# New tables for a planned order: half-width turns of three blocks, earlier and later ranks of weight conversions, twelve tiles with their rests by identity products

## The chip, the cores and the metric

The kernel runs on one core of one Trainium2 chip. The metric is the device time of one execution in microseconds (us). In the rows PE is TensorE, PEld is TensorE's loading of stationary operands, DVE is VectorE, ACT is ScalarE, POOL is GpSimd and SP is SyncE, which issues all the transfers here.

## What is computed

An attention of the mLSTM kind (a recurrence with a matrix state) over 4 sequences of 768 steps with 8 heads of width 40 gives 3072 rows of 320 numbers. Two dense layer pairs of inner width 2048 follow, each with its own pointwise function.

```python
def _attn_ref(q, k, v, i_gate, f_gate, o_gate):      # per step t
    m_new = np.maximum(f_gate[:, :, t] + m, i_gate[:, :, t])
    C = f_stab[:, :, None, None] * C + i_stab[:, :, None, None] * np.einsum('bhd,bhe->bhde', vt, kt)
    ...
    y[:, :, t] = o * h_tilde / denom

def _moe_ref(x, w_in, w_out):
    h = x @ w_in                    # 3072x320 @ 320x2048
    g = np.where(h >= 1, h, np.where(h <= -1, 0.0, (h + 1) ** 2 / 4))
    return g @ w_out                # 3072x2048 @ 2048x320

def _moe2_ref(x, w_in, w_out):
    h = x @ w_in
    g = np.maximum(h, 0.0) ** 2
    return g @ w_out
```

## The kernel before

**Tiling.** The 3072 rows are cut into 24 chunks of 128. The attention of a chunk needs the state of the chunk before it in the same sequence. Chunks are put together to blocks: for the first dense pair (part 0) three blocks of two chunks and six of three (`SIZES1`), for the second (part 1) eight of three. The inner width 2048 is 16 tiles of 128 (`f` from 0 to 15). One visit is a block with one `f`: `mm1` (L694) makes `h`, ScalarE and VectorE make the activation (L699, L705, L712), its value is split into a rounded part `g0` (L270) and a rest `g1` (L722), and `mm2` (L747) adds the block's products with the output weights to one accumulator per chunk.

**Weights.** They arrive as 64-bit floats, one transfer of 704 KB per tile and part (`raw`, L284), and become a float32 in five steps: `a_abs` on ScalarE (L288), then four VectorE instructions (L296, L297, L301, L309). `a_hi` (L270) writes the rounded weights. Their rest, the float32 less the rounded value, is made in one of two ways. Either VectorE makes it by two subtractions (`v_lo` L318 and `lo` L322, the latter sometimes on GpSimd). Or, for the tiles of part 0 that are named in `PLO`, TensorE makes it in two halves (`plo`, L345): the float32 by an identity matrix (L350), less the rounded value by a negated identity (L351), in an accumulator from which ScalarE copies (L270).

**Order.** Nothing is ordered by hand. Each step is handed to a planner (`Plan`) with its engine or a choice of engines, a rank, a cost, what it needs and what it makes; the planner plays the program through with these costs, takes the ready step of lowest rank on each engine, and the instructions are issued in the order that comes out. On each engine they then run in that order. Tables of numbers set the ranks:

- `TURNS1` and `TURNS2`: in what order some blocks take ranges of `f`. A block that leaves off in the middle of the width keeps its partial sums in `pa` (`keep`, and L762 where there are sums already) and adds them at the end (L775).
- `AT`: ranks of the first six attentions; `LEAD1`: how many visits ahead of a block its later attentions stand.
- `WAT`: ranks of the 16 weight conversions of part 0; `WLEAD2`: how many visits ahead of their use those of part 1 stand, for `f` under 8 and from 8 on.
- `GATE`: rank of the gates of the later chunks. The first six attentions (`SPR`) get their decay factors by a spread on TensorE (L504), the others by a transfer (`fb`).
- `GLOV`: blocks whose `g1` is made on VectorE; for the others the planner chooses between GpSimd and VectorE.
- `wraw`, `d0`, `d1` in `bufs`: how many buffers the raw weights and the decay matrices have.
- `FILL`: 140 products of zeros (L815) of lowest rank, which the planner puts where TensorE has nothing else to do.

Of the attention, L509 is the scan that makes a decay matrix `d`, L537 the scores, L518 the scores times `d`, L572 the outer products, L582 and L586 the state, L609 and L613 the reading of the state and of the scores, L633 the result `xn`, L652 and L662 its transpose and the rest of its rounding.

## Time and profile before

| what | us |
|---|---|
| median of three runs | 897.83 (895.91 to 904.17) |
| the profiled execution, its own time | 893.81 |
| its span, first to last instruction | 892.0 |
| TensorE's matmuls busy in the span | 873.6 (98%) |
| TensorE's weight loads busy | 850.4 (95%) |
| VectorE, ScalarE, GpSimd busy | 451.9, 451.5, 390.0 |

A busy time is the time covered by an engine's instructions in the profile. Matmuls overlap and their ends are modelled, so that a busy TensorE need not be at its peak. A row of a window gives the busy time of each engine in it, with the number of instructions, and the granted share of TensorE's clock.

### The profile page before, as it was taken

The page shows a single profiled execution, that of the slowest core. Times are in us where ns is not written, and L with a number is a line of the kernel's source. Part 1 is how long each engine was busy: PE and PEld are TensorE (multiplying, and loading weights), DVE is VectorE, ACT ScalarE, POOL GpSimd, SP SyncE. Part 2 cuts the span into 40 slices and gives each one's busy share as a digit, 9 for nine tenths or more (in the row PEclk, how much of TensorE's full clock was granted, in tenths as well). Part 3 has the DMA queues.
Part 4 walks back from the last instruction along what each step waited for, and adds up shares of the span by engine and source line. Part 5 has one row for each costly group of instructions (what it writes and reads, how often), then busy time and mean ns, then how long its engine had stood idle before and what let it go on. Part 6 is the DMA issues. An engine that isn't in the chain of part 4 may idle for free.

```text
span 892.0 us, 15463 instructions
## 1 busy us (share of the span) xinstructions
PE 873.6 (98%) x5922; PEld 850.4 (95%) x5922; DVE 451.9 (51%) x806; ACT 451.5 (51%) x973; POOL 390.0 (44%) x383
## 2 busy tenths in 40 slices
PE   8889999999999999999999999999999999999997
PEld 7768999999999999999999999999999999999997
DVE  5798898864535444454528888722222222211221
ACT  5256596555454554544468675543344444333433
POOL 3221433465646555555435556533333333333333
PEclk7699999999999999999999999999999999999999
DMA  7654445373233233343102332001101010000000
GB/s 234 201 193 147 151 144 166 114 208 105 88 108 113 94 118 100 98 130 101 51 1 70 134 127 87 1 18 39 34 25 34 22 38 10 23 12 12 16 9 22
DMA packets 55981, 75.74 MB, mean 85 GB/s; under 512 B 7252, under 2 KB 44792, under 8 KB 55908
## 3 DMA queue, kind: packets, MB, share of 16 engines
q1 hardware_dynamic: 55908, 74.77, 26.4%
q8 instruction: 46, 0.75, 0.4%
q14 instruction: 27, 0.22, 0.1%
HBM read 65.90 MB, written 8.85 MB: 84 GB/s over the span
## 4 chain that ended last, share of the span: by engine, by line
PE 90%; DVE 5%; ACT 2%; issue 1%; DMA 1%; POOL 1%; DVEq 0%; ACTq 0%; POOLq 0%
PE h L694 38%; PE acc L747 36%; PE v L613 4%; PE s L537 3%; PE v L572 2%; PE s L504 2%; PE s L652 2%; PE v L609 1%; PE acc L815 1%; PE acc L350 1%; DVE wt L301 1%; DVE wt L296 1%; DVE r L712 1%; DVE wt L309 1%; ACT r L699 1%
## 5 line engine op out<-in xcount | busy, mean ns | idle before, releaser
L722 POOL TENSOR_TENSOR g<-r,g 128x384 fp32r<-128x384 f32 (+1 forms) x256 | 262.4, 1026 | 368.9 <-ACT g L270 292.4
L747 PE MATMUL acc<-w,g 128*128 128x320 f32 x2304 | 380.5, 311 | 0.7 <-POOL g L722 0.5
L694 PE MATMUL h<-xTh,w 128*128 128x384 f32 (+1 forms) x1360 | 356.9, 331 | 2.8 <-DVE r L712 2.3
L747 PEld LDWEIGHTS acc<-w,g 128*128 128x128 f32 x2304 | 349.6, 188 | 4.5 <-POOL g L722 1.2
L694 PE MATMUL h<-xTl,w 128*128 128x384 f32 (+1 forms) x816 | 266.5, 327 | 0.0
L694 PEld LDWEIGHTS h<-xTh,w 128*128 128x128 f32 x1360 | 242.7, 188 | 6.5 <-DVE r L712 4.9
L270 ACT ACTIVATE g<-r 128x384 fp32r<-128x384 f32 (+1 forms) x272 | 136.2, 503 | 108.4 <-DVE r L714 61.0
L714 DVE TENSOR_TENSOR r<-r,h 128x384 f32<-128x384 f32 x128 | 70.6, 553 | 236.8 <-ACT r L701 236.8
L694 PEld LDWEIGHTS h<-xTl,w 128*128 128x128 f32 x816 | 153.9, 189 | 0.0
L699 ACT ACTIVATE r<-h,half 128x384 f32<-128x384 f32 (+1 forms) x144 | 78.2, 543 | 117.3 <-PE h L694 114.3
L701 ACT ACTIVATE r<-h 128x384 f32<-128x384 f32 x128 | 62.6, 489 | 137.3 <-PE h L694 99.3
L712 DVE SCALAR_TENSOR_TENSOR r<-r,h 128x384 f32<-128x384 f32 (+1 forms) x144 | 72.3, 503 | 91.1 <-ACT r L705 87.3
L705 ACT ACTIVATE r<-r 128x384 f32<-128x384 f32 (+1 forms) x144 | 70.0, 486 | 3.0
L509 DVE TENSOR_TENSOR_SCAN d<-fb,csb 128x512 f32<-128x512 f32 x36 | 48.6, 1349 | 33.8 <-PE v L613 31.5
L544 POOL TENSOR_TENSOR vt<-vko,it 128x369 f32<-128x369 f32 x24 | 28.9, 1206 | 61.9 <-PE v L613 49.3
L613 PEld LDWEIGHTS v<-vt,d 128*128 128x128 f32 x384 | 49.4, 198 | 1.0 <-DVE C L582 0.4
L613 PE MATMUL v<-vt,d 128*128 128x41 f32 x384 | 49.1, 279 | 0.2 <-DVE C L582 0.2
L518 DVE TENSOR_TENSOR d<-s,d 128x512 f32<-128x512 f32 x48 | 31.0, 674 | 18.3 <-PE s L537 18.3
L301 DVE SCALAR_TENSOR_TENSOR wt<-wraw,wt 128x704 int32<-128x704 int32 x32 | 37.4, 1172 | 0.2
L309 DVE SCALAR_TENSOR_TENSOR wt<-wraw,wt 128x704 int32<-128x704 int32 x32 | 33.9, 1058 | 0.1
L537 PE MATMUL s<-qk 40*128 40x128 f32 x384 | 32.1, 303 | 1.2 <-DVE rc L623 1.0
L288 ACT ACTIVATE wt<-wraw 128x704 f32<-128x704 f32 x32 | 27.0, 844 | 11.4 <-DMA wraw<-in_wts_dram 4.5
(73 smaller groups left out, 633.8 us busy)
## 6 DMA issues: line engine op xcount, KB each, us to landing
wraw<-in_wts_dram SPq DMA_DIRECT2D x32, 704.0 KB
vko<-in_vko_dram SPq DMA_DIRECT2D x24, 524.5 KB
fb<-f SPq DMA_DIRECT2D x18, 512.0 KB
qk<-in_qk_dram SPq DMA_DIRECT2D x48, 160.0 KB
x<-x SPq DMA_DIRECT2D x24, 192.0 KB
x<-o SPq DMA_DIRECT2D x24, 160.0 KB
out_dram<-o SPq DMA_DIRECT2D x24, 160.0 KB
qh<-in_qh_dram SPq DMA_DIRECT2D x20, 180.0 KB
```

The lines of the kernel that those rows point to most:

```text
L270: nc.scalar.activation(out=out, in_=in_, func=ACTF.Copy)
L509: nc.vector.tensor_tensor_scan(out=d.rearrange("p h t -> p (h t)"), data0=(z["fb"][a] if spr else z["fb"][:, 4 * a:4 * a + 4]).rearrange(" ...
L537: nc.tensor.matmul(out=z["s", a][:, h], lhsT=z["qk"][r, 0, h], rhs=z["qk"][r, 1, h], start=True, stop=True)
L613: nc.tensor.matmul(out=z["y"][:, E * h:E * (h + 1)], lhsT=z["d", a][:, h - 4 * a], rhs=z["vt"][:, h], start=(h == 0 and c == 0), stop=True ...
L694: nc.tensor.matmul(out=h, lhsT=a, rhs=b, start=(i == 0), stop=(i == 7))
L699: nc.scalar.activation(out=r, in_=z["h"], func=ACTF.Relu, scale=0.5, bias=half)
L701: nc.scalar.activation(out=r, in_=z["h"], func=ACTF.Relu)
L705: nc.scalar.activation(out=z["r"], in_=z["r"], func=ACTF.Square)
L712: nc.vector.scalar_tensor_tensor(out=r, in0=r, scalar=1.0, in1=z["h"], op0=ALU.min, op1=ALU.max)
L714: nc.vector.tensor_mul(out=r, in0=r, in1=z["h"])
L722: engine[e].tensor_sub(out=z["g1"], in0=z["r"], in1=z["g0"].bitcast(F32))
L747: nc.tensor.matmul(out=acc[k][:, 0:DM], lhsT=a, rhs=b, start=(f == f0 and i == 0), stop=(f == f1 - 1 and i == 2))
```

## The change

Tables alone are changed in effect. The first three blocks take their turns by eight `f` and no longer by four, so that a block leaves off once and not three times. The ranks of the first attentions, of the conversions and of the gates move. `PLO` goes from the 8 even tiles to 12. The `g1` of blocks 1, 2 and 3 is made on VectorE, that of block 0 where the planner chooses. Raw weights have three buffers, not four, and the decay matrices two, not one. `EARLY` is 0, so that the new places it selects (`xy`, the tag `h`) are not taken, and a spread's tile keeps its shape.

```diff
-TURNS1 = [(0, 0, 4), (1, 0, 4), (0, 4, 8), (1, 4, 8), (2, 0, 4), (2, 4, 8),
-          (0, 8, 12), (1, 8, 12), (2, 8, 12), (0, 12, 16), (1, 12, 16), (2, 12, 16)]
+TURNS1 = [(0, 0, 8), (1, 0, 8), (2, 0, 8), (0, 8, 16), (1, 8, 16), (2, 8, 16)]
...
-AT = [-20, -16, -8, -4, 4, 8]
-WAT = [-14, -13, -12, -11, -3, -2, -1, 0, 11, 12, 13, 14, 20, 21, 22, 23]
-LEAD1 = {3: [12, 8, 4], 4: [12, 8, 4], 5: [12, 8, 4], 6: [12, 8, 4], 7: [12, 8, 4], 8: [8.5, 6, 3.5]}
+AT = [-21.0, -17.0, -5.5, -3.0, 3.5, 6.5]
+WAT = [-14, -13.0, -13, -6, -3, 0, 2, 2.5, 9.5, 17.5, 16.5, 25.0, 27.0, 27.0, 31.5, 32.0]
+LEAD1 = {3: [12.5, 8, 3.5], 4: [13.5, 5.5, 3.5], 5: [13.5, 10, 7.0], 6: [13, 6.5, 2.5], 7: [13, 11, 3.0], 8: [7.5, 5, 2.5]}
...
-GATE = -14
+XTB, PAB = 3, 6
+RAWB, DB = 3, 2
+EARLY = 0
+GATE = -19
...
-PLO = range(0, 16, 2)
-WLEAD2 = (10, 10)
+PLO = (0, 1, 2, 3, 4, 6, 8, 10, 11, 12, 13, 14)
+WLEAD2 = (13, 6)
...
-GLOV = (0,)
+GLOV = (1, 2, 3)
...
-        wraw=4, wt=3, qk=2, vko=2, fb=1, qh=2, ab=2, d0=1, d1=1,
+        wraw=RAWB, wt=3, qk=2, vko=2, fb=1, qh=2, ab=2, d0=DB, d1=DB,
```

In the changed file the lines stand one or two further down: L296 is L297, L301 is L302, L712 is L714, L694 is L696.

The first place is VectorE's queue ahead of the first activation of a dense visit (`r<-r,h`). Before, these are the rows up to it, with the conversion of a seventh tile (`wt_582`) and of an eighth (`wt_662`):

```order
L518 TENSOR_TENSOR d1_684<-s_696,d1_684 128x512
L633 TENSOR_TENSOR xn_716<-v_657,sg_409 128x320
L309 SCALAR_TENSOR_TENSOR wt_582<-wraw_511,wt_582 128x704
L296 TENSOR_SCALAR wt_662<-wt_662 128x704
L297 TENSOR_SCALAR wt_662<-wt_662 128x704
L582 TENSOR_TENSOR C_741<-v_720,csb_84 120x369
L662 TENSOR_TENSOR xTl_737<-s_726,xTh_736 128x3x128
L301 SCALAR_TENSOR_TENSOR wt_662<-wraw_558,wt_662 128x704
L712 SCALAR_TENSOR_TENSOR r_591<-r_591,h_571 128x256
```

In the changed kernel the same activation has these rows ahead of it, with the sixth tile (`wt_541`) as the last, and the seventh (`wt_603`) behind it:

```order
L310 SCALAR_TENSOR_TENSOR wt_541<-wraw_496,wt_541 128x704
L511 SCALAR_TENSOR_TENSOR d0_646<-s_623,csb_81 128x512
L511 SCALAR_TENSOR_TENSOR d1_657<-s_641,csb_81 128x512
L319 TENSOR_TENSOR w5_655<-wt_541,w5_655 64x128
L323 TENSOR_TENSOR w5_655<-wt_541,w5_655 128x576
L625 TENSOR_SCALAR rc_684<-v_650 128x8
L626 TENSOR_TENSOR rc_684<-v_650,rc_684 128x8
L627 RECIPROCAL rc_684<-rc_684 128x8
L714 SCALAR_TENSOR_TENSOR r_586<-r_586,h_563 128x256
...
L297 TENSOR_SCALAR wt_603<-wt_603 128x704
```

Two conversions, among other rows, have moved from ahead of the first activation to behind it.

The second place is TensorE's queue behind the fourth visit of block 0. Before, block 1 begins with tile 0 there (its transposed input is `xTh_736`):

```order
L747 MATMUL acc0_789<-w2_489,g0_834 128x320 x2
L747 MATMUL acc0_789<-w2_489,g1_845 128x320
L504 MATMUL s_854<-w11_122,csb_84 128x128 x4
L747 MATMUL acc1_795<-w2_489,g0_834 128x320 x2
L747 MATMUL acc1_795<-w2_489,g1_845 128x320
L694 MATMUL h_869<-xTh_736,w0_381 128x256
```

In the changed kernel block 0 (`xTh_415`) goes on with tile 4 instead, and ahead of it stand products of zeros and an identity half of tile 6:

```order
L696 MATMUL h_798<-xTh_415,w3_526 128x256 x2
L696 MATMUL h_798<-xTl_416,w3_526 128x256
L817 LDWEIGHTS x2_125
L817 MATMUL acc2_131<-x2_125 128x160
L817 LDWEIGHTS x2_125
L817 MATMUL acc2_131<-x2_125 128x160
L351 MATMUL acc2_131<-wt_603,csb_81 128x352
L352 MATMUL acc2_131<-w6_809,nident_82 128x352
...
L696 MATMUL h_836<-xTh_415,w4_608 128x256
```

Of the 140 products of zeros all stand ahead of the first visit before, and 118 in the changed kernel; the other 22 stand between the first and the ninth.

The third place is SP's queue of transfers, where the raw weights of tiles 0 to 2 have been asked for. Before, the load of tile 3 (`wraw_335`) stands behind the inputs of the third attention:

```order
L463 DMA qk_302<-in_qk_dram 40x2x512 x2
L467 DMA vko_317<-in_vko_dram 128x1049
L284 DMA wraw_335<-in_wts_dram 128x1408
L436 DMA a1_91<-w10_123 36x640
L476 DMA qh_372<-in_qh_dram 120x384
L463 DMA qk_376<-in_qk_dram 40x2x512 x2
L467 DMA vko_392<-in_vko_dram 128x1049
```

In the changed kernel it (`wraw_397`) stands behind those of the fourth too:

```order
L465 DMA qk_299<-in_qk_dram 40x2x512 x2
L469 DMA vko_311<-in_vko_dram 128x1049
L437 DMA a1_88<-w10_120 36x640
L478 DMA qh_338<-in_qh_dram 120x384
L473 DMA fb_342<-f1_87 128x8x128
L465 DMA qk_362<-in_qk_dram 40x2x512 x2
L469 DMA vko_379<-in_vko_dram 128x1049
L285 DMA wraw_397<-in_wts_dram 128x1408
```

The load of tile 3 has moved behind five more transfers.

## Rows read from the trace of the kernel before

**Rows 1.** Windows, by stage: busy us of PE, PEld, DVE, ACT, POOL, then granted clock

```profile
0.00:40.00 40.00, 35.33 (x215) 30.71 (x215) 25.31 (x44) 16.59 (x30) 11.15 (x15) 0.66 0.65 209
40.00:80.00 40.00, 34.10 (x241) 28.40 (x240) 36.51 (x67) 22.21 (x48) 9.93 (x10) 0.91 0.63 198
80.00:200.00 120.00, 118.57 (x930) 113.44 (x931) 102.67 (x196) 75.64 (x193) 52.40 (x59) 1.00 0.49 153
200.00:600.00 400.00, 398.13 (x2731) 391.33 (x2731) 220.34 (x376) 221.35 (x463) 211.34 (x195) 1.00 0.27 86
600.00:892.00 292.00, 287.43 (x1811) 286.46 (x1809) 67.05 (x125) 115.67 (x241) 105.20 (x104) 1.00 0.07 23
```

**Rows 2.** Timeline of ScalarE and VectorE, first 200 us: start us, us, instruction

```profile
52.12 0.48 ACT L699 ACTIVATE r<-h,half 128x256 f32<-128x256 f32 x1
...
71.13 0.41 DVE L712 SCALAR_TENSOR_TENSOR r<-r,h 128x256 f32<-128x256 f32 x1
...
197.18 0.42 DVE L712 SCALAR_TENSOR_TENSOR r<-r,h 128x256 f32<-128x256 f32 x1 [1.61 <-ACT r L705]
```

**Rows 3.** Groups of VectorE by line and shape, first 200 us: count | busy, mean ns | idle before

```profile
L301 DVE SCALAR_TENSOR_TENSOR wt<-wraw,wt 128x704 int32<-128x704 int32 x19 | 20.3, 1070 | 0.1
...
L309 DVE SCALAR_TENSOR_TENSOR wt<-wraw,wt 128x704 int32<-128x704 int32 x19 | 18.6, 980 | 0.0
L509 DVE TENSOR_TENSOR_SCAN d<-s,csb 128x512 f32<-128x512 f32 x12 | 14.7, 1223 | 9.0 <-PE s L504 5.4 <-PE v L613 3.6
L518 DVE TENSOR_TENSOR d<-s,d 128x512 f32<-128x512 f32 x20 | 12.9, 681 | 3.3 <-PE s L537 3.3
L296 DVE TENSOR_SCALAR wt<-wt 128x704 f32<-128x704 f32 x19 | 12.2, 642 | 0.0
L297 DVE TENSOR_SCALAR wt<-wt 128x704 int32<-128x704 int32 x19 | 12.1, 635 | 0.7
...
L722 DVE TENSOR_TENSOR g<-r,g 128x256 fp32r<-128x256 f32 x16 | 8.6, 536 | 1.2 <-ACT g L270 1.2
L322 DVE TENSOR_TENSOR w<-wt,w 128x576 fp32r<-128x576 f32 x8 | 7.0, 874 | 0.1
L762 DVE TENSOR_TENSOR pa<-acc,pa 128x320 f32<-128x320 f32 x12 | 5.4, 487 | 0.6 <-PE acc L747 0.6
L586 DVE SCALAR_TENSOR_TENSOR cx<-C,ab,v 120x123 f32<-120x123 f32 x18 | 5.1, 338 | 0.4 <-PE v L572 0.4
L662 DVE TENSOR_TENSOR xTl<-s,xTh 128x384 fp32r<-128x384 f32 x9 | 5.0, 551 | 0.6 <-ACT xTh L270 0.6
...
L318 DVE TENSOR_TENSOR w<-wt,w 64x128 fp32r<-64x128 f32 x8 | 3.2, 401 | 0.2
```

**Rows 4.** Chain that ended last, in order of time: start us, us, what

```profile
57.00 0.78 PE acc L350 x2
57.78 0.16 PE acc L351
...
94.13 0.95 PE h L694 x8
...
97.32 0.59 PE acc L350 x2
97.91 0.16 PE acc L351
```

**Rows 5.** Timeline of SP and ScalarE: loads of tiles 1 and 2, a `qk` load, first uses

```profile
7.83 0.45 SPq L284 DMA_DIRECT2D wraw<-in_wts_dram  x1
...
16.43 0.35 SPq L284 DMA_DIRECT2D wraw<-in_wts_dram  x1
...
31.93 1.60 SPq L463 DMA_DIRECT2D qk<-in_qk_dram  x2
...
17.11 0.86 ACT L288 ACTIVATE wt<-wraw 128x704 f32<-128x704 f32 x1 [0.81 <-DMA wraw<-in_wts_dram]
21.68 0.84 ACT L288 ACTIVATE wt<-wraw 128x704 f32<-128x704 f32 x1 [3.72 <-DMA wraw<-in_wts_dram]
```

More of the change, by code (lines that the diff above doesn't have):

```diff
@@ L197 @@
     bufs.update(
-        wraw=4, wt=3, qk=2, vko=2, fb=1, qh=2, ab=2, d0=1, d1=1,
-        ws=2, vt=2, qt=2, kt=2, sg=2, xn=2, rc=2, cx=1, C=5, xT=XTB, pa=6, r=3, g0=3, g1=3, o=2, x2=2,
+        wraw=RAWB, wt=3, qk=2, vko=2, fb=1, qh=2, ab=2, d0=DB, d1=DB,
+        ws=2, vt=2, qt=2, kt=2, sg=2, xn=2, rc=2, cx=1, C=5, xT=XTB, pa=PAB, r=3, g0=3, g1=3, o=2, x2=2,
         h=2, acc0=1, acc1=1, acc2=1, s=2, v=1)
@@ L452, in gate_part, with attention @@
         plan.add(A, rank, act(R * (c1 - c0)), cp, [("s", ("it", c0))], [("it", c) for c in range(c0, c1)])
-    def attention(n, at, spr):
+    def attention(n, at, spr, early=0):
+        xy = "acc0" if early > 1 else "v"
         b, c = divmod(n, NCB)
@@ L501, in spread @@
                 z["fb"] = z.get("fb") or {}
-                z["fb"][a] = t = new("s", [128, 4, L])
+                z["fb"][a] = t = new("h" if early else "s", [128, 512 // L, L])
                 for h in range(4):
@@ L521, in attention @@
             if spr:
-                fk = ("s", ("fb", n, a))
+                fk = ("h" if early else "s", ("fb", n, a))
                 plan.add(T, at - 7 + a, 0.92, spread, [(f"w{NF - 5}", 0, min(c, 1), 1)], [fk])
@@ L569, in outer @@
         def outer():
-            z["x"] = x = new("v", [128, 512])
+            z["x"] = x = new(xy, [128, 512])
             for i in range(3):
@@ L596, in attention @@
             plan.add(pv(HP * D), at - 4, 0, k_in, [("vko", n), ("ws", n, 0), ("ws", n, 1)], [("kt", n)])
-            plan.add(T, at - 2.5, 0.66, outer, [("kt", n), ("vt", n)], [("v", ("x", n))])
+            plan.add(T, at - 2.5, 0.66, outer, [("kt", n), ("vt", n)], [(xy, ("x", n))])
             if c == 0:
-                plan.add(V, at - 2, dvep(HP * E), update, [("v", ("x", n))], [("C", n)])
+                plan.add(V, at - 2, dvep(HP * E), update, [(xy, ("x", n))], [("C", n)])
             else:
-                plan.add(V, at - 2, 3 * 0.34, update, [("v", ("x", n)), ("C", n - 1), ("ab", n)], [("cx", n)])
+                plan.add(V, at - 2, 3 * 0.34, update, [(xy, ("x", n)), ("C", n - 1), ("ab", n)], [("cx", n)])
                 plan.add(pv(HP * E), at - 1, 0, mask, [("cx", n)], [("C", n)])
@@ L605, in read @@
             if a == 0:
-                z["y"] = new("v", [128, 512])
+                z["y"] = new(xy, [128, 512])
                 if c:
@@ L616, in attention @@
         plan.add(T, at - 1, 0.9 + (0.67 if c else 0), lambda: read(0),
-                 [("d0", n, 1), ("vt", n)] + ([("qt", n), ("C", n - 1)] if c else []), [("v", ("y", n))])
-        plan.add(T, at - 0.9, 0.9, lambda: read(1), [("d1", n, 1), ("vt", n), ("v", ("y", n))], [("v", ("y", n), 1)])
+                 [("d0", n, 1), ("vt", n)] + ([("qt", n), ("C", n - 1)] if c else []), [(xy, ("y", n))])
+        plan.add(T, at - 0.9, 0.9, lambda: read(1), [("d1", n, 1), ("vt", n), (xy, ("y", n))], [(xy, ("y", n), 1)])
         def norm_a():
@@ L633, in norm_c @@
             nc.vector.tensor_mul(out=xn[:, 0:DM].rearrange("p (h e) -> p h e", e=D), in0=y[:, :, 0:D], in1=z["sg"])
-        plan.add(V, at, 0.55, norm_a, [("v", ("y", n), 1)], [("rc", n)])
+        plan.add(V, at, 0.55, norm_a, [(xy, ("y", n), 1)], [("rc", n)])
         plan.add(pv(DM), at + 0.1, 0, norm_b, [("rc", n), ("sg", n)], [("sg", n, 1)])
@@ L638, in again @@
             nc.scalar.activation(out=z["xn"][:, DM:384], in_=z["xn"][:, 256:DM], func=ACTF.Copy)
-        plan.add(V, at + 0.2, dvep(DM), norm_c, [("v", ("y", n), 1), ("sg", n, 1)], [("xn", n, 0)])
+        plan.add(V, at + 0.2, dvep(DM), norm_c, [(xy, ("y", n), 1), ("sg", n, 1)], [("xn", n, 0)])
         plan.add(A, at + 0.3, act(64), again, [("xn", n, 0)], [("xn", n)])
@@ L837 @@
                 m += 1
-                attention(n, at, m <= SPR)
+                attention(n, at, m <= SPR, m if m <= EARLY else 0)
                 to_xT(j, k, lambda n=n: t_["z", n]["xn"], at)
```

1 line of the change is left out of this document (removed).

## The prediction

> **What bounds the kernel now.** I read the windows by stage first. From 200 us on TensorE is full: its weight loads alone cover 391.33 of 400 us and then 286.46 of 292 [rows 1]. No table can win more there than the 8.7 and 5.5 us that are left, part of which is the store at the end. From 80 to 200 us its weight loads cover 113.44 of 120 us, so that at most 6.6 us are free, while VectorE is at 102.67. The room is ahead of that: in the first 80 us the weight loads cover 30.71 and 28.40 us, 59.1 of 80, and part of this is the 140 products of zeros and work at a granted clock of 0.66 and 0.91 [rows 1].
>
> The timeline of VectorE and ScalarE says why dense work starts late. ScalarE begins the first activation at 52.12 us, and VectorE's step of it, the gate, begins at 71.13 [rows 2]. Those 19 us are not a wait for data. VectorE is busy for 36.51 of the 40 us from 40 to 80 [rows 1], and the step stands behind conversions in its queue. So VectorE's queue bounds the start, and TensorE everything from about 80 us on. The 48th gate, the last of the three small blocks, begins at 197.18 [rows 2]. The time of the kernel moves by what that point moves, and it is the earlier of the two only if VectorE's queue and TensorE's work both allow it.
>
> **The change on VectorE.** I counted what stands in VectorE's queue ahead of a given gate in the two orders and priced the difference by the groups of the first 200 us [rows 3].
>
> Ahead of the first gate there are two instructions less of each of L296, L297, L301, L318, L322 and L518, one less of L309, L582, L633 and L662. That is 2 x (0.642 + 0.635 + 1.070 + 0.401 + 0.874 + 0.681) + 0.980 = 9.6 us, and three of about 0.5 us (L662 is 0.551, taken for all three: 1.6): **11.2 us less**.
>
> Ahead of the fourth there is one less of each of the four conversion steps (3.3), three less of L318 and L322 (3.8), three less of L722 (1.6) and one less of L662 (0.6), against two scans more (2.4): 6.9 us less. Ahead of the eighth: one less of L296, L297 and L301 (2.3), two less of L318 and L322 (2.6), four less of L722 (2.1), three more of L586 (1.0): **6.0 us less**. Ahead of the 48th: four less of L318 and L322 (5.1), twelve less of L762 (5.8) and three less of L586 (1.0), against 15 more of L722 (8.0) and two more scans (2.4): 1.5 us less. So the lead is large at first and VectorE gives it back, because `g1` of blocks 1 and 2 is now its work and block 0 runs through eight tiles, whose conversions have to come one after the other.
>
> A second buffer for the decay matrices ends a wait. Of the 9.0 us that the early scans wait, 3.6 are for L613, TensorE's reading of the matrix before [rows 3]. This bounds the saving at 3.6 us. The other 5.4, for the spread on TensorE, stay. Where a scan starts earlier, the next wait is for the same spread or for a load, so I take 2.0.
>
> **The change on TensorE.** Four tiles more have their rests by identity products, two halves each. A half takes 0.59 + 0.16 = 0.75 us with nothing in between, and 0.78 + 0.16 = 0.94 where other work runs into it [rows 4]. I take 0.75, since TensorE is dense where they count. Eight halves are 6.0 us (7.5 by the other row). Where they stand matters: 8 halves ahead of the first visit, not 4, and there TensorE plays products of zeros, so four of the eight are hidden. After the eighth visit 12 halves are left, not 8. So four halves, **3.0 us**, are on the path. Further, the new order has nine first products behind it at the eighth visit's last product, the old one ten: one of 0.95 us [rows 4] is still ahead, **1.0 us**.
>
> ScalarE copies each half from the accumulator, 4 tiles more. It is at 75.64 of 120 us from 80 to 200 [rows 1], so I cost that at nothing. If its queue were the cover that fails, each copy would sit ahead of a dense visit's first step, and the price is in the range. The products of zeros that now stand among the dense visits, 22 of them, fall where the order leaves TensorE a gap, and I cost them at nothing too. GpSimd loses the `g1` of two blocks and gets that of one; at 52.40 of 120 us it waits for others anyway [rows 1].
>
> The other tables move attentions and part 1's conversions within the stretch from 200 to 600 us, where VectorE is at 220.34 of 400 and TensorE full [rows 1]. I take nothing for that, with 2 us either way. The clock's share of 0.91 from 40 to 80 us amounts to 40 x 0.09 = 3.6 us lost; if the changed order keeps TensorE busier there, part of it comes back, and one more idle stretch of this kind would cost as much. I take nothing and put it into the range.
>
> **The sum.** The eighth gate is the point that I choose: ahead of it VectorE's queue decides, behind it TensorE's work. It gives -6.0 + 3.0 + 1.0 = -2.0, and with -2.0 for the decay buffers -4.0 us. The profiled execution took 893.8 us (span 892.0, and 1.8 around it), so it would take 889.8. It lay 4.0 us below the median of the runs, 897.8, and a run is what is predicted: **893.8 us**. Ends of this case: had VectorE bound as late as the 48th gate, whose lead is 1.5 us, with no help from the buffers, the four halves could cost a little more than is won, +2 us; with the fourth gate's 6.9, the whole 3.6 and no halves in the way, -8.
>
> **Rivals.**
>
> *The whole lead passes.* If TensorE has enough to do from the first gate on, the 11.2 us count in full: -11.2 + 3.0 - 3.6 = -11.8 us, 886.0. For it: TensorE is at 98.8% in the window behind (118.57 of 120 [rows 1]), so it could use earlier work. Against it: block 0 must wait there for tiles 4 to 7, which block 1 needed not in the old order, and the 22 products of zeros stand just there.
>
> *The products are paid in full.* If the first visits begin no earlier, because another step of the start (a spread, a load) ends last, the path has all eight halves: +6.0 us, 903.8. The trace is against it, since VectorE's queue and not the data held the first gate for 19 us [rows 2]. A rule speaks for it: the Trainium skill, "Perfetto Trace Analysis", section "Identifying the Most-Contended Engine", says to judge TensorE by the share of its weight loads and to relieve the most contended engine first. By that rule TensorE is the engine to spare and the change loads it; the trace agrees from 200 us on, and not in the first 80.
>
> *Slower: raw weights come late.* With three raw buffers, and the load of tile 3 behind the `qk` and `vko` of the fourth attention, it is asked for only after a `qk` that went out at 31.93 us. The load of tile 2 took from 16.43 to its first use at 21.68, 5.2 us; that of tile 1, with more transfers beside it, from 7.83 to 17.11, 9.3 us [rows 5]. A buffer is held for the load, the first step (0.86 [rows 5]) and the four VectorE steps (3.3 [rows 3]) with about as much other VectorE work between them: 5.2 + 0.9 + 6.6 = 12.7 us, a tile every 4.2 us from three buffers; at 9.3 us 16.8, a tile every 5.6. The old order takes its eight tiles in the time to about 75 us, some 5 us each. So loads under about 7.5 us are hidden and longer ones are not; if they stay at 9.3, 0.6 us or more for each of 13 tiles, and since VectorE's queue holds all behind the waiting conversion, scans and gates too, up to 1 us each: +8 to +13, 910 at the far end. Against it: after the start, few rows show ScalarE waiting for a load.
>
> **How the numbers follow.** A run of this kernel can tell about 1%, 9 us, from no change. The forecast has 0.60, the whole lead 0.20, the products in full 0.12, late weights 0.08. The forecast's own range is 890 to 900. To hold 8 in 10 it is widened to the whole lead with the clock's gain on one side and to the products in full on the other: 884 to 903. Faster by over 1% (under 888.9) come 0.18 from the whole lead and 0.04 from the forecast's edge: 0.22. Slower (over 906.8) come 0.07 from late weights and 0.02 from products at 0.94: 0.09. The rest is 0.69.
>
> **What would show it.** Right: VectorE's first gate near 60 us, the fourth near 72, the 48th near 193; no L762 in the first 200 us; 48 rows of the identity products at L350's place and 24 at L351's; from 200 us on the same windows. The eighth gate no more than 6 us earlier, with TensorE idle or on products of zeros between the fourth and the eighth, would confirm where the lead goes. Wrong: a first gate later than 67 us; ScalarE's first weight step waiting for `wraw` over and over (late weights); a 48th gate near 186 (the whole lead); or a stretch behind 200 us that differs by more than 2 us, which no term here has.

## The result and the profile after

| | before | changed |
|---|---|---|
| median of 13 runs each, us | 897.71 (893.85 to 905.51) | 890.65 (885.61 to 904.04) |
| ratio, with its 95% interval | | 0.9912 [0.9882, 0.9941] |
| the profiled execution, us | 893.81 | 892.52 |
| its span, us | 892.0 | 890.7 |

The medians are over all runs; a ratio and its interval leave out runs more than 1.5% above the fastest of their kernel, such as the one of 904.04 us, so that the two need not agree to the last digit. The changed kernel is faster by 0.6 to 1.2%, 5 to 11 us. The predicted time was 893.8 us, with 4.0 us gained. The two profiled executions differ by 1.3 us only: the one before was short for its kernel, the one after was not. So what one trace says of the start is a single draw, and the experiments had to tell the rest.

The windows of the changed kernel, in the columns of [rows 1]:

```profile
0.00:40.00 40.00, 36.00 (x220) 32.39 (x221) 26.24 (x44) 16.17 (x30) 10.83 (x15) 0.66 0.68 208
40.00:80.00 40.00, 37.09 (x246) 29.98 (x246) 30.07 (x53) 20.03 (x49) 12.06 (x13) 0.87 0.49 160
80.00:200.00 120.00, 120.00 (x945) 114.69 (x944) 103.80 (x207) 81.24 (x209) 40.65 (x41) 1.00 0.53 168
200.00:600.00 400.00, 398.94 (x2743) 392.89 (x2742) 232.07 (x394) 220.39 (x461) 202.23 (x180) 1.00 0.28 85
600.00:890.70 290.70, 286.06 (x1802) 285.04 (x1800) 65.73 (x122) 115.22 (x240) 105.36 (x104) 1.00 0.07 23
```

From 40 to 80 us VectorE went from 36.51 busy us to 30.07 and TensorE from 34.10 to 37.09 [rows 1]: VectorE is no longer the full engine there. Its timeline says what it waits for (in brackets the idle time ahead and what ended it):

```profile
48.10 1.22 DVE L511 TENSOR_TENSOR_SCAN d<-s,csb 128x512 f32<-128x512 f32 x1 [0.43 <-PE s L506]
...
54.18 1.22 DVE L511 TENSOR_TENSOR_SCAN d<-s,csb 128x512 f32<-128x512 f32 x1 [2.34 <-PE s L506]
...
59.55 1.29 DVE L520 TENSOR_TENSOR d<-s,d 128x512 f32<-128x512 f32 x2 [2.56 <-PE s L539]
...
67.02 0.37 DVE L714 SCALAR_TENSOR_TENSOR r<-r,h 128x256 f32<-128x256 f32 x1
...
80.36 0.41 DVE L714 SCALAR_TENSOR_TENSOR r<-r,h 128x256 f32<-128x256 f32 x1
...
196.98 0.41 DVE L714 SCALAR_TENSOR_TENSOR r<-r,h 128x256 f32<-128x256 f32 x1
```

The rows of L714 are the first, the fourth and the 48th gate. The first came 4.1 us earlier than before, the 48th 0.2 [rows 2]; the fourth came at 80.36, against 78.92 before. Two waits of 4.9 us together, for a spread (L506) and for scores (L539), stand ahead of the first. The chain that ended last says why these were late (start us, us, what):

```profile
38.36 6.46 DMA wraw<-in_wts_dram
...
48.06 0.79 PE acc L351 x2
49.91 0.69 PE acc L817 x4
50.60 1.25 PE acc L351 x2
52.14 2.00 PE s L506 x8
54.15 1.47 PE acc L351 x2
55.91 1.37 PE h L696 x8
57.36 1.00 PE h L696 x8
```

The spread of eight products took 2.00 us here and takes 1.08 at 46.97 and at 61.12 us of the same chain. The windows around it show TensorE's clock:

```profile
44.00:50.00 6.00, 4.38 (x27) 2.81 (x27) 4.83 (x8) 3.85 (x10) 1.14 (x1) 0.99 0.81 259
50.00:57.00 7.00, 7.00 (x26) 5.35 (x25) 3.97 (x6) 1.92 (x5) 0.00 (x0) 0.52 0.01 4
```

From 50 to 57 us the granted clock was 0.52, the lower of the two levels (1.2 GHz, not 2.4), just when TensorE had the spread and the first dense visit to do. Ahead of that, from 44 to 50, it had been busy for 4.38 of 6 us. Before the change such a stretch lay from 64 to 71 us, at 0.53.

The groups of VectorE for the first 200 us that answer to [rows 3]:

```profile
L724 DVE TENSOR_TENSOR g<-r,g 128x256 fp32r<-128x256 f32 x32 | 14.9, 464 | 5.2 <-ACT g L271 4.9
L511 DVE TENSOR_TENSOR_SCAN d<-s,csb 128x512 f32<-128x512 f32 x12 | 14.7, 1221 | 10.3 <-PE s L506 6.8 <-DMA vko<-in_vko_dram 3.3
...
L323 DVE TENSOR_TENSOR w<-wt,w 128x576 fp32r<-128x576 f32 x4 | 3.0, 757 | 0.0
```

The scans' wait of 3.6 us for L613 is gone, as a second buffer should make it. But their waits sum to 10.3 us and not to 9.0: a load of `vko` (3.3) and a longer wait for the spread took its place. The identity products came as counted:

```profile
L351 PE MATMUL acc<-wt,csb x48: 457/459/953, 36.2 to 145.5; 128*128 128x352 f32 x48
L352 PE MATMUL acc<-w,nident x24: 587/592/1015, 36.5 to 145.6; 128*128 128x352 f32 x24
```

For the raw weights the timeline of ScalarE has one wait behind 40 us, at the fifth tile, and the chain one piece of 6.46 us (the first line of the chain above), the load of that tile:

```profile
44.84 0.86 ACT L289 ACTIVATE wt<-wraw 128x704 f32<-128x704 f32 x1 [0.63 <-DMA wraw<-in_wts_dram]
```

That load began at 38.36 on SP and landed 6.5 us later, between the 5.2 and the 9.3 of [rows 5]. ScalarE's wait is short, but the load is part of the chain that ended last: it is on the path to the first gate. The chain before has no load between 28 and 72 us. The same holds across the experiments below. Of the nine profiles with three raw buffers eight have a raw load of 5.9 to 9.6 us in the chain there (all but e15); of the five with four buffers (before, e1, e3, e5, e14) none has (e5 has another load, of `ab`). In e0, the same program as the changed kernel, it is the fourth tile's load, 8.3 us, and ScalarE waits longer for it:

```profile
32.67 8.30 DMA wraw<-in_wts_dram
...
41.00 0.83 ACT L289 ACTIVATE wt<-wraw 128x704 f32<-128x704 f32 x1 [2.99 <-DMA wraw<-in_wts_dram]
```

The chain there goes on from the load to this step. Before, the fourth tile's load was asked for at 20.36 us, ahead of need; with three buffers it waits for a buffer that VectorE gives back, and is asked for at 32.67 here and at 33.70 in the changed kernel's profile.

### The profile page after: what moved, and what is told of

Read it like the earlier page. It is cut to its first block, busy times and chain, and to the rows that moved or that the text cites. A ratio compares the mean times of both kernels' runs of the same rounds, so it can differ in the third digit from the quotient of the medians.

```text
span 890.7 us, 15443 instructions
## 1 busy us (share of the span) xinstructions
PE 878.1 (99%) x5946; PEld 855.0 (96%) x5946; DVE 457.9 (51%) x817; ACT 453.1 (51%) x985; POOL 371.1 (42%) x352
## 4 chain that ended last, share of the span: by engine, by line
PE 95%; DMA 2%; ACT 1%; DVE 1%; issue 1%; POOL 0%; SPq 0%; DVEq 0%; ACTq 0%
PE h L696 40%; PE acc L749 38%; PE v L615 4%; PE s L539 3%; PE s L506 2%; PE s L654 2%; PE v L574 2%; PE acc L351 1%; PE v L611 1%; PE acc L817 1%; DMA wraw<-in_wts_dram 1%; DMA w<-in_gates_dram 0%; PE acc L352 0%; DMA x<-o 0%; ACT r L701 0%
## 5 line engine op out<-in xcount | busy, mean ns | idle before, releaser
L724 POOL TENSOR_TENSOR g<-r,g 128x384 fp32r<-128x384 f32 (+1 forms) x224 | 240.1, 1074 | 317.4 <-ACT g L271 283.1
L696 PE MATMUL h<-xTh,w 128*128 128x384 f32 (+1 forms) x1360 | 357.7, 331 | 0.4 <-DVE r L714 0.4
L696 PE MATMUL h<-xTl,w 128*128 128x384 f32 (+1 forms) x816 | 267.4, 328 | 0.0
L696 PEld LDWEIGHTS h<-xTh,w 128*128 128x128 f32 x1360 | 243.8, 189 | 2.1 <-DVE r L714 1.0
L696 PEld LDWEIGHTS h<-xTl,w 128*128 128x128 f32 x816 | 154.5, 189 | 0.0
L714 DVE SCALAR_TENSOR_TENSOR r<-r,h 128x384 f32<-128x384 f32 (+1 forms) x144 | 72.6, 504 | 84.2 <-ACT r L707 77.0
L568 POOL TENSOR_TENSOR kt<-vko,ws 128x360 f32<-128x360 f32 x20 | 18.1, 903 | 62.1 <-ACT ws L517 62.1
L546 POOL TENSOR_TENSOR vt<-vko,it 128x369 f32<-128x369 f32 x24 | 20.6, 860 | 42.2 <-PE v L615 29.3
L302 DVE SCALAR_TENSOR_TENSOR wt<-wraw,wt 128x704 int32<-128x704 int32 x32 | 36.1, 1127 | 0.2
L594 POOL TENSOR_TENSOR C<-cx,csb 120x369 f32<-120x369 f32 x16 | 15.0, 936 | 49.6 <-DVE cx L588 42.2
```

The source lines that it names most:

```text
L302: nc.vector.scalar_tensor_tensor(out=t, in0=z["raw"][:, :, 0], scalar=29, in1=t, op0=ALU.logical_shift_right, op1=ALU.bitwise_or)
L696: nc.tensor.matmul(out=h, lhsT=a, rhs=b, start=(i == 0), stop=(i == 7))
L714: nc.vector.scalar_tensor_tensor(out=r, in0=r, scalar=1.0, in1=z["h"], op0=ALU.min, op1=ALU.max)
L724: engine[e].tensor_sub(out=z["g1"], in0=z["r"], in1=z["g0"].bitcast(F32))
```

## The experiments

Three theories stood against each other. **S**: the gain is made at the start, by VectorE's shorter queue there (the prediction's). **L**: it is made behind 200 us, by the ranks of the late conversions and attentions. **C**: the 22 products of zeros that the new order puts among the first visits keep TensorE's clock up. Every ratio is to the kernel before on the same chip, timed in the same series, and its median there was 898.29 us for e1 to e4, 896.45 for e0, e5, e6 and e11, 898.28 for e12 to e14 and 899.25 for e15; medians of different series are not to be compared. The gates are those of one profiled execution each:

| kernel | ratio [95%] | gate 1 | 4 | 8 | 48 | clock 0-40, 40-80 |
|---|---|---|---|---|---|---|
| before | 1 | 71.1 | 78.9 | 97.9 | 197.2 | 0.66, 0.91 |
| changed | 0.9912 [0.9882, 0.9941] | 67.0 | 80.4 | 97.5 | 197.0 | 0.66, 0.87 |
| e0, changed again | 0.9955 [0.9914, 0.9996] | 66.4 | 79.9 | 97.0 | 196.5 | 0.74, 0.87 |
| e1, new turns alone | 1.0002 [0.9964, 1.0039] | 75.7 | 83.4 | 101.7 | 200.8 | none, 0.83 |
| e2, old `PLO` | 0.9989 [0.9951, 1.0028] | 68.3 | 86.6 | 95.7 | 197.0 | 0.74, 0.83 |
| e3, old `GLOV` and buffers | 1.0013 [0.9984, 1.0041] | 61.7 | 82.8 | 101.2 | 201.1 | none, 0.91 |
| e4, old ranks | 1.0004 [0.9971, 1.0037] | 75.0 | 86.8 | 98.1 | 205.9 | 0.66, 0.78 |
| e5, old buffers | 0.9962 [0.9919, 1.0005] | 63.6 | 76.8 | 92.1 | 200.9 | 0.66, 0.83 |
| e6, old late ranks | 0.9934 [0.9898, 0.9970] | 67.0 | 80.3 | 97.5 | 197.0 | 0.70, 0.87 |
| e11, 118 products | 1.0033 [0.9991, 1.0076] | 75.7 | 104.1 | 119.4 | 214.6 | none, 0.67 |
| e12, without the 22 | 0.9944 [0.9912, 0.9976] | 66.8 | 79.9 | 100.2 | 199.5 | 0.70, 0.87 |
| e13, the 22 tripled | 0.9999 [0.9958, 1.0039] | 65.3 | 81.0 | 102.7 | 202.5 | none, 0.86 |
| e14, before, 260 products | 0.9974 [0.9944, 1.0005] | 70.0 | 77.9 | 96.9 | 196.5 | 0.87, 0.87 |
| e15, more ahead, none among | 0.9866 [0.9818, 0.9914] | 63.5 | 76.4 | 93.6 | 193.0 | 0.83, 0.96 |

"None" stands where the profile has no record of the clock for most or all of that stretch (its first is at 33 to 41 us) and its window reads 1.00 for want of one. The products contradict this reading: the spread of eight takes as long in e13 (the second pair of rows) as in the changed kernel (the first), where the clock is on record at 0.52:

```profile
8.00:30.00 22.00, 21.82 (x122) 19.47 (x124) 14.49 (x20) 10.03 (x17) 6.53 (x7) 0.52 0.71 227
10.77 2.08 PE L506 MATMUL s<-w,csb 36*128 36x128 f32 x8
...
8.00:30.00 22.00, 21.73 (x118) 19.35 (x118) 14.07 (x17) 10.18 (x17) 6.14 (x6) 1.00 0.74 228
11.43 2.07 PE L506 MATMUL s<-w,csb 36*128 36x128 f32 x8
```

The other profiles lack the record for their first 4 to 6 us, so that their figures for 0 to 40 us are a little too high.

Each edit to a table makes the planner order everything anew. So e1 to e6 and e11 compare whole orders; e12, e13 and e15 alone keep the order of the other work.

**e1, the new turns alone** in the kernel before.

```diff
-TURNS1 = [(0, 0, 4), (1, 0, 4), (0, 4, 8), (1, 4, 8), (2, 0, 4), (2, 4, 8),
-          (0, 8, 12), (1, 8, 12), (2, 8, 12), (0, 12, 16), (1, 12, 16), (2, 12, 16)]
+TURNS1 = [(0, 0, 8), (1, 0, 8), (2, 0, 8), (0, 8, 16), (1, 8, 16), (2, 8, 16)]
```

> The kernel before with the new turns of the first three blocks, and nothing else. Theory S (the gain is made at the start, by what stands ahead of the first eight gates in VectorE's queue): the queue is the same up to the eighth gate, then 12 additions of partial sums are gone (5.8 us of VectorE, most of it beside TensorE's work), so 0 to 3 us faster than before, ratio 0.997 to 1.000. Theory L (the gain is made behind 200 us, by the ranks of the later attentions and of part 1's conversions): 1.000. If the turns themselves are the gain: 0.991.

Measured: 897.57 us, ratio 1.0002, no gain. The turns alone, in the old order's other tables, are worth nothing.

**e2, the old tiles with identity products**, the rest as changed.

```diff
-PLO = (0, 1, 2, 3, 4, 6, 8, 10, 11, 12, 13, 14)
+PLO = range(0, 16, 2)
```

> The changed kernel with 8 tiles' rests by identity products, not 12. TensorE has 6.0 us less to do, VectorE 5.1 us more. If TensorE bounds from the first visits on: 3 to 6 us faster than the changed kernel, ratio to the kernel before 0.985 to 0.988. If VectorE's queue bounds there: up to 5 us slower than the changed kernel, 0.991 to 0.997. Theory L: TensorE's 6 us count, 0.985.

Measured: 898.35 us, ratio 0.9989, and no gain is left to see, though eight halves (6.0 us) have left TensorE. Against the changed kernel's 0.9912 that is a loss; the interval [0.9951, 1.0028] overlaps that of its second timing (e0). Its profiled execution is one of its shortest runs (891.32), and in it the fourth gate is 6.2 us late and the first 1.3; where the other runs lose their time, no trace shows.

**e3, the old blocks with `g1` on VectorE and the old buffers**, the rest as changed. The expectation speaks of the first alone, but the kernel that ran has both, so that it is to be read against e5, which undoes the buffers, and not against the changed kernel.

```diff
-GLOV = (1, 2, 3)
+GLOV = (0,)
...
-        wraw=RAWB, wt=3, qk=2, vko=2, fb=1, qh=2, ab=2, d0=DB, d1=DB,
+        wraw=4, wt=3, qk=2, vko=2, fb=1, qh=2, ab=2, d0=1, d1=1,
```

> The changed kernel with the rests g1 of block 0 on VectorE and those of blocks 1 to 3 where the planner chooses, as before. VectorE has about 8 us less ahead of the 48th gate, GpSimd more. Theory S: where VectorE gives the lead back between the eighth and the 48th gate, 2 to 5 us faster than the changed kernel, 0.986 to 0.989. If TensorE alone bounds there: the same as the changed kernel, 0.991. If GpSimd's longer step (0.84 against 0.54 us) delays the second products: 0.993 or more.

Measured: 898.1 us, ratio 1.0013, the gain is gone, by the two edits together. Over e5 (0.9962) the loss is 0.5% and the intervals overlap, so what `GLOV` alone is worth is not shown. VectorE has less to do (94.27 busy us from 80 to 200, against 103.80) and the first gate is the earliest of all (e5's, with the same buffers, is 1.9 us later), but the eighth and the 48th are 4 us later than in the changed kernel. GpSimd makes 31 of the first visits' `g1` again at 0.840 us each (16 in the changed kernel); VectorE takes 0.464.

**e4, the old ranks** of attentions, conversions and gates, the rest as changed.

```diff
-AT = [-21.0, -17.0, -5.5, -3.0, 3.5, 6.5]
-WAT = [-14, -13.0, -13, -6, -3, 0, 2, 2.5, 9.5, 17.5, 16.5, 25.0, 27.0, 27.0, 31.5, 32.0]
+AT = [-20, -16, -8, -4, 4, 8]
+WAT = [-14, -13, -12, -11, -3, -2, -1, 0, 11, 12, 13, 14, 20, 21, 22, 23]
...
-GATE = -19
+GATE = -14
```

`LEAD1` and `WLEAD2` were put back too.

> The changed kernel with the old ranks (first attentions, conversions of both parts, later attentions, gates); new turns, 12 tiles by identity products, g1 and buffers stay. Theory S: VectorE's lead at the first gate falls from 11 to 3 us while TensorE keeps the 6.0 us more, so the gain is lost or turned round: 0.998 to 1.005. Theory L: lost too, 0.999 to 1.002, but the windows up to 200 us would be as in the changed kernel. If turns, buffers and identity products make the gain: 0.991.

Measured: 898.62 us, ratio 1.0004, the gain is gone; the first gate is at 75.0 and the 48th at 205.9, both later than before the change (its clock from 40 to 80 us, 0.78, is one of the lowest, which the gates include). The other new tables without these ranks gain nothing.

**e0, the changed kernel again**, unchanged.

> The changed kernel again, unchanged, for a second profile beside the experiments. Theory S: where the first profile shows the 48th gate no earlier than the kernel before does (196.98 against 197.18 us), other executions have it 3 to 8 us earlier, as the medians differ by 7 us. Theory L: every execution has the 48th gate near 197 and makes its gain behind it. Ratio 0.988 to 0.994.

Measured: 892.96 us, ratio 0.9955. The gain is there again, smaller. Two timings of one kernel differ by 0.4%, so single experiments are read to that and no finer. The 48th gate is at 196.5, not the 3 to 8 us earlier that was expected of theory S: this profile does not show the place of the gain either.

**e5, the old buffers**, the rest as changed (both edits undone as one).

```diff
-RAWB, DB = 3, 2
+RAWB, DB = 4, 1
```

> The changed kernel with four raw-weight buffers and one buffer for each decay matrix, as before. The scans wait again for the reading of the matrix before (up to 3.6 us); loads may start earlier (tile 3's first weight step waited 0.63 us for its load). Theory S: 1 to 4 us slower than the changed kernel, 0.992 to 0.996. If the late loads of three raw buffers cost more than the decay buffers give: faster than the changed kernel, 0.985 to 0.990.

Measured: 898.73 us, ratio 0.9962 [0.9919, 1.0005]. Between the changed kernel and no gain, and not settled: 0.1 to 0.5% above the changed kernel's two ratios, 0.6 to 4.5 us. (But for one of 906.08, its runs fall in two groups, five from 890.2 to 894.3 us and six from 898.66 to 900.66, so that the median lies above that of the kernel before in its series, 896.45, and the ratio below 1.) In its profile the first, fourth and eighth gates are earlier than in the changed kernel's (63.6, 76.8, 92.1) and the 48th is 3.9 us later.

**e6, the old late ranks**, the rest as changed: the old `LEAD1` and `WLEAD2`.

```diff
-LEAD1 = {3: [12.5, 8, 3.5], 4: [13.5, 5.5, 3.5], 5: [13.5, 10, 7.0], 6: [13, 6.5, 2.5], 7: [13, 11, 3.0], 8: [7.5, 5, 2.5]}
+LEAD1 = {3: [12, 8, 4], 4: [12, 8, 4], 5: [12, 8, 4], 6: [12, 8, 4], 7: [12, 8, 4], 8: [8.5, 6, 3.5]}
...
-WLEAD2 = (13, 6)
+WLEAD2 = (10, 10)
```

> The changed kernel with the old ranks of the later attentions and of part 1's conversions alone; the first attentions, part 0's conversions and the gates keep their new ranks, and VectorE's queue up to the 48th gate has the same work. Theory S: the gain stays, 0.990 to 0.993, at most 2 us of it lost. Theory L: the gain goes, 0.998 to 1.000, with the windows behind 200 us longer.

Measured: 891.49 us, ratio 0.9934, the gain between those of the changed kernel's two timings. Theory L falls: the late ranks do not make it.

**e11, 118 products of zeros** in the changed kernel, just those that stand ahead of the first visit.

```diff
-FILL, FDUR = 140, 0.2
+FILL, FDUR = 118, 0.2
```

> The changed kernel with 118 products of zeros, not 140, so that none is left to stand among the first eight visits. Theory S (work in VectorE's queue): they stand in gaps of TensorE, 0.990 to 0.993. Theory C (what the change gains is that TensorE is kept busy among the first visits, so that its clock is seldom at 1.2 GHz there): the gain goes, 0.996 to 1.000, and the runs scatter as those of the kernel before do.

Measured: 903.18 us, ratio 1.0033 [0.9991, 1.0076], all gain lost; that it is slower than before is not shown. (Its profiled execution, 911.71 us, is its longest run; the gates in the table are read with that.) Theory C seemed shown. But the edit does a second thing: the planner's time runs on without those 22, and it sets other steps in their place. By a count like the prediction's VectorE has some 10 us more ahead of its fourth gate than in the changed kernel, a further conversion among it. Its windows, in the columns of [rows 1]:

```profile
40.00:80.00 40.00, 31.70 (x167) 24.53 (x166) 22.87 (x40) 16.84 (x38) 9.09 (x10) 0.67 0.47 150
80.00:200.00 120.00, 119.14 (x844) 112.55 (x842) 95.22 (x185) 73.97 (x188) 38.25 (x38) 0.91 0.46 147
```

**e12, e13: the 22 alone.** The planner still plans them, so that on VectorE, ScalarE, GpSimd and the DMA queues every instruction stands where it stood. e12 issues none of them (the first line with +), e13 each three times (the second).

```diff
-        plan.add(T, -97 if i == 0 else 1e6, 0.22 if i < 30 else FDUR, lambda i=i: idle(i == 0),
+        plan.add(T, -97 if i == 0 else 1e6, 0.22 if i < 30 else FDUR, lambda i=i: idle(i == 0) if i < 118 else None,
+        plan.add(T, -97 if i == 0 else 1e6, 0.22 if i < 30 else FDUR, lambda i=i: [idle(i == 0) for _ in range(1 if i < 118 else 3)],
```

> The changed kernel in which the last 22 products of zeros, those that stand among the first visits, issue nothing; everything else stands in the same order. Theory C (those products keep TensorE's clock up through the first visits): the gain is lost, ratio to the kernel before 0.996 to 1.003, the granted clock of the stretch from 40 to 80 us at or under 0.75 in the profile, the 48th gate at 200 us or later. Theory S (the gain is VectorE's shorter queue at the start, and the products only fill waits): ratio 0.990 to 0.994 as the changed kernel, or a little under it, since 22 products of about 0.07 to 0.13 us leave TensorE's queue.

> The changed kernel in which each of the same 22 products of zeros is issued three times, all into the same bank, 44 products more on TensorE between the first visits. Theory C: ratio 0.986 to 0.992, as good as the changed kernel or better, with less scatter among the runs. Theory S: the 44 products are paid where TensorE is the engine waited for, 44 x 0.07 to 0.13 us, 3 to 6 us at most, so ratio 0.992 to 0.998.

Measured: e12 894.12 us, ratio 0.9944, within the two ratios of the changed kernel. The 22 products are worth nothing that two timings 0.4% apart can tell, and theory C, as far as it is about them, falls; what e11 lost, it lost by the order. e13: 899.84 us, 5.7 us over e12 by the medians and 0.55% (4.9 us) by the ratios, for 66 products more: 0.07 to 0.09 us each, against a median of 0.098 us for the weight load of one in its profile. The scatter of the runs leaves about 3.6 us either way, so that this fits products paid in full and does not measure the price. Neither theory had e13 so slow (0.9999; 0.998 at most was expected).

Here a rule of the Trainium skill bears out that I put among the rivals ("Perfetto Trace Analysis", section "Identifying the Most-Contended Engine": judge TensorE by its weight loads). From 57 to 101 us, where the 66 stand in e13, TensorE was the engine to spare: in the changed kernel its weight loads cover 39.73 of those 44 us, and VectorE is busy for 37.44.

**e14, the kernel before with more products of zeros**, 251 ahead of the first visit and 9 among the visits. The order of all else is as it was but for a few neighbours on VectorE and ScalarE early on; VectorE's work ahead of each gate in the table is the same.

```diff
-FILL, FDUR = 140, 0.2
+FILL, FDUR = 260, 0.1
```

> The kernel before with more and shorter-spaced products of zeros (FILL, FDUR = 260, 0.1 in place of its own): 251 ahead of the first visit and 9 among the visits, the order of the other work as in the kernel before. Theory C: faster than the kernel before, ratio 0.992 to 0.997, the long stretch at half clock ahead of 40 us shorter or gone and the 48th gate at 193 to 196 us. Theory S: ratio 0.998 to 1.002, since no engine's queue of work is changed; slower, up to 1.01, if the 120 products more hold back the scores of the first visit.

Measured: 895.48 us, ratio 0.9974 [0.9944, 1.0005]. Not told from no change. Its runs may lie closer: 892.67 to 902.3 for 12 runs, against 893.22 to 911.83 for the 29 of the kernel before in that series, but 29 runs reach further than 12 of themselves.

**e15, the version that the runs point to**: the changed kernel without the 22, and with 88 of the 118 ahead of the first visit issued twice.

```diff
-        plan.add(T, -97 if i == 0 else 1e6, 0.22 if i < 30 else FDUR, lambda i=i: idle(i == 0),
+        plan.add(T, -97 if i == 0 else 1e6, 0.22 if i < 30 else FDUR, lambda i=i: [idle(i == 0) for _ in range(1 if i < 30 else 2 if i < 118 else 0)],
```

> The changed kernel without the 22 products of zeros among the first visits, and with 88 of the 118 ahead of the first visit issued twice; VectorE's, ScalarE's, GpSimd's and the DMA queues' order unchanged. Theory S (the gain is the order on VectorE; products of zeros among the visits are paid and worth nothing): ratio 0.990 to 0.995 as without the 22. If products of zeros ahead of the first visit help as they seemed to in the kernel before (0.9974 there): 0.985 to 0.990, the granted clock ahead of 40 us at 0.85 or over in the profile. Theory C as first put (those among the visits are needed): 0.996 to 1.003.

Measured: 888.36 us, ratio 0.9866 [0.9818, 0.9914], six runs between 883.1 and 889.42. Its interval lies clear of 1 and its ratio is the best of all; over the changed kernel (0.9912) its lead is not beyond both intervals, over e12 (0.9944) it all but is. The clock ahead of 40 us, 0.83, is just under the 0.85 that was to go with it. Its windows around the start, and its chain there:

```profile
44.00:50.00 6.00, 5.04 (x41) 3.73 (x41) 4.77 (x6) 3.93 (x9) 1.48 (x1) 1.00 0.60 190
50.00:57.00 7.00, 7.00 (x57) 5.86 (x55) 4.72 (x7) 4.45 (x12) 0.84 (x1) 1.00 0.25 80
```

```profile
51.02 1.09 PE s L506 x8
52.10 0.79 PE acc L351 x2
53.05 1.90 PE h L696 x16
54.95 1.09 PE s L539 x16
```

TensorE is busier ahead of 50 us (5.04 of 6), its clock stays at the upper level from 50 to 57, and the spread takes 1.09 us, not 2.00. The first two visits' products end at 54.95, against 58.36 in the changed kernel, whose chain has them from 55.91 on. No load is in this chain from 30 to 72 us. VectorE's gates follow:

```profile
52.14 1.22 DVE L511 TENSOR_TENSOR_SCAN d<-s,csb 128x512 f32<-128x512 f32 x1 [0.69 <-PE s L506]
...
56.14 1.29 DVE L520 TENSOR_TENSOR d<-s,d 128x512 f32<-128x512 f32 x2 [1.19 <-PE s L539]
...
63.53 0.37 DVE L714 SCALAR_TENSOR_TENSOR r<-r,h 128x256 f32<-128x256 f32 x1
...
193.04 0.41 DVE L714 SCALAR_TENSOR_TENSOR r<-r,h 128x256 f32<-128x256 f32 x1
```

The same two waits are 1.9 us and not 4.9. The first gate is 3.5 us earlier than in the changed kernel, and in this pair of profiles all of it is kept: the fourth is 4.0 earlier, the eighth 3.9, the 48th 3.9, the span 4.2 us shorter. So 3 to 4 us at the start were worth 4 us at the end, with the same order and no further loss of clock behind. e12 shows the other case: its fourth gate is 0.5 us earlier than the changed kernel's, its clock from 85 to 100 us is 0.77, and its eighth gate is 2.7 us later.

## Why the prediction was right, and where it was not

**The sign and the size held, the place in part.** The gain needs the early ranks: it goes with all the ranks (e4) and stays without the late ones (e6). It is also gone without the new tiles of `PLO` (e2, against one of two timings) and without the new `GLOV` and buffers (e3). Theory S stands so far, with three things open. None of the runs isolates how much of it is VectorE's queue and how much TensorE's, since each table moves both. No profile of the changed order but e15's has the 48th gate earlier by more than 0.8 us; in the pair before and changed the 1.3 us are made behind it (below). And part of the 7 us between the medians may be that fewer runs lose clock at the start, which no run tests. The likeliest case, 4.0 us, was small: the four timings of the changed order (with e0, e6 and e12) give 0.9912 to 0.9955, 4 to 8 us.

**The first gate failed** (67.0, "wrong if later than 67"; near 60 was expected). The 11.2 us did leave VectorE's queue, but 7 of them turned into waiting, and the step that failed is "VectorE's queue bounds the start" with nothing named as next. (The chain of the kernel before spoke against it already: from 40 us to the first gate it runs 16 us on TensorE and 13 on VectorE.) With the conversions gone, two things are next. One is a load of raw weights, which the sum had at nothing (a rival took loads under about 7.5 us as hidden): 6.5 us of it are in the changed kernel's chain, 8.3 in e0's. The other is TensorE's spread and scores behind it, at a clock for which I took nothing. Five more profiles have this order of VectorE's queue at the start. In e0, e6 and e12 ScalarE waits 2.6 to 3.0 us for the load, TensorE has at most 0.22 us of products from 40 to 43 us, and the clock is 0.51 to 0.53 from 43 to 50; the gate is at 66.4 to 67.0, although the spreads behind 50 us run at the upper level. In e13 the wait is 0.81 us, the clock from 43 to 50 is 0.76, and the gate at 65.3. In e15 there is neither, TensorE is busy for 2.45 of the 3 us, and the gate is at 63.5:

```profile
40.00:43.00 3.00, 0.00 (x0) 0.00 (x0) 1.10 (x2) 1.97 (x3) 1.54 (x2) 0.98 0.77 235
43.00:50.00 7.00, 6.21 (x24) 4.02 (x24) 3.99 (x7) 3.18 (x9) 1.41 (x2) 0.52 0.77 249
50.00:57.00 7.00, 6.26 (x41) 4.80 (x41) 5.55 (x8) 3.35 (x9) 0.00 (x0) 1.00 0.01 2
...
40.00:43.00 3.00, 2.45 (x22) 1.68 (x21) 2.79 (x5) 1.43 (x3) 2.67 (x3) 1.00 0.92 292
43.00:50.00 7.00, 5.29 (x44) 3.85 (x42) 5.77 (x8) 4.66 (x11) 1.73 (x1) 1.00 0.65 210
```

(e0, then e15.) So the load and the lower clock that comes with it are worth about 3.5 us of the 7 together; no run separates them, and that the wait brings the clock down is argued from the order in time.

**The fourth gate failed** (80.4, near 72 expected), and load and clock are not all of that, since e15 has it at 76.4. I counted TensorE's additions at the eighth visit alone. Counted at the last output product of the fourth, TensorE has four halves (3.0 us), the spread for one of an attention's two matrices (8 records in the trace at 0.11 us, 0.9), eight readings of scores (16 records, 1.8) and three of the state (6 records, 0.7) more and one first product (0.95) less: 5.4 us more, against VectorE's 6.9 less. (At the eighth the prediction's count of halves still to come, 12 against 8, holds at the gate; at the last output product, where it counts the first products, it is 12 against 7.) The two take turns waiting for each other there, and neither queue alone gives the gate.

**The eighth and the 48th.** The sum put its -4.0 us at the eighth gate and the 48th "near 193". In the changed kernel's profile they are 0.4 and 0.2 us earlier, a miss; in e15, where the load is not in the chain and the clock is at the upper level from 33 to 63 us, 4.3 earlier and at 193.0. This agrees with the sum, but e15 has also other products, and it is one execution.

**The halves: the price held, the balance did not.** 48 and 24 rows and no L762 in the first 200 us came as predicted. Undoing `PLO` should by my terms have changed little at the eighth gate: 3.0 us back on TensorE, two more subtractions of each kind (2.6) on VectorE. Measured, it costs 0.3 to 0.8% (the first within the noise), with all the rest planned anew. That VectorE's two subtractions for a tile are worth more than TensorE's halves is one reading, not shown. Likewise `GLOV`: I booked 15 more of L722 (8.0 us) as a loss of VectorE's lead. Undoing it on top of the buffers (e3 against e5) gains nothing and may cost 0.5%. That the activation's way over GpSimd at 0.840 us, and not VectorE's load, is what that choice set would fit e3's groups; no run measures it.

**The decay buffers.** -2.0 us of a bound of 3.6 was taken. The wait went, another of 3.3 came in the profile, and e5 gives 0.6 to 4.5 us together with the raw buffers. The term is neither refuted nor settled.

**Products of zeros at nothing: right.** e12 shows it for the 22, to 0.4%; e13 shows that more of them are not free there.

**The other rivals.** The whole lead did not pass (48th gate at 197.0, not 186). Raw weights did come late in part. ScalarE waits for them once (0.63 us; 2.99 in e0) and not "over and over", and nothing near +8 us came of it, but the rival's doubt was right: the load is on the path to the first gate. Behind the 48th gate nothing differs by more than 2 us to the end of the span (694.8 before, 693.7 after), as costed. But within it the profile moved more: from gate 129 to 137 it went from 25.7 us to 21.3, and gave 2.0 back by gate 145. Gate 129 is 0.9 us later than before, gate 145 1.5 earlier: the 1.3 us between the two profiles are made here. e1 and e14 have the old 25.7 us, and every other profile 19.7 to 21.3, also those with the old late ranks (e4, e6), the old `PLO`, `GLOV` or buffers. So undoing one table does not undo it and the turns alone do not bring it; no cause was shown.

**From one execution to the median.** I added 4.0 us because the profiled execution lay so far below the median. That made 893.8 of 889.8; the measured median, 890.65, lies between. That the measured time came out so near is in part luck: the 4.0 us of the forecast stand against 1.3 between the two profiles and 7.1 between the two medians.

## What to carry to other kernels

When work leaves the queue of the engine that bounds a stretch, count what is queued on the next engine at the same point and not further down: here VectorE's 11.2 us turned into 4.1 because a load and TensorE's spread and scores were next. Follow the chain, too, and not only the waits: a load with 0.63 us of waiting at its user had 6.46 us on the path. A planner's tables can't be tested one by one, nor its fillers by their number, since all that follows is planned anew: keep the plan and change only what is issued. Compare an experiment's whole kernel with the one it is meant to differ from (e3 undid more than was meant). Where executions differ by 1% from run to run, compare the spread of runs, and not one trace with one trace.

## What the runs showed of the hardware

I had not expected that one program's executions differ in where TensorE's lower clock falls in the first 110 us, and that this shows in the gates. With the order of VectorE's queue the same, the clock from 43 to 50 us was 0.52 in e0, 0.99 in the changed kernel (which has 0.52 from 50 to 57 instead), 0.76 in e13 and 1.00 in e15. Behind 100 us it is at the upper level in all of them to the last few us. The first gate was at 66.4, 67.0, 65.3 and 63.5. So some 7 us at 1.2 GHz ahead of the first gate go with 2.9 to 3.5 us at the gate, wherever in these 14 us they fall, the waiting ahead of them included. One such stretch further on, in e12 (0.77 from 85 to 100 us), goes with 2.7 us at the eighth gate.

Times of many runs come in steps: for the kernel before, in the series of e12 to e14, five runs took 896.0 to 896.5 us, all at a mean granted clock of 0.976, and three 894.7 to 895.1 at 0.995. But the mean does not order the runs: at 0.982 three took 893.2, 902.2 and 905.0 us, and at 0.986 e0 has one of 887.55 and one of 900.14. And it can't be taken at its word, since a profile without a record for the start counts that start at 1.00 (e1, e3, e11 and e13, where the products ran at the lower level). So comparing kernels at like mean clock, tempting as the steps make it, is not safe. Tried on e15 it does not give one number either: against runs of the kernel before within 0.002 of the same mean, four of e15's are 10 to 12 us faster and two (889.3 and 889.4 at 0.994) 5.5.

The Trainium skill, "TensorE: Matmul & The Clock Gate", section "Part 1: The HAM clock gate", says that an idle TensorE falls to 1.2 GHz. The rows agree with the levels and with idleness ahead of the fall: e0's clock fell at 43 us behind 3 us without a product, and the changed kernel's at 50 us behind a stretch with 4.38 of 6 us busy, against 5.04 in e15, where it did not fall. What decides it from run to run of the same program no run here shows; that the landing of a load has a part in it is argued above.
